# A linear-attention block feeding a GELU MLP on one core: state decay applied block by block, diagonals of the first units by selector matmuls, and a new instruction order

## The chip, the cores and the metric

One core of one Trainium2 chip. The metric is the time of one execution in device microseconds (us). The kernel before takes 191.64 us, the median of 3 runs (191.53 to 192.08). A program on one core has no second core to compare with, so "slow" here is only said of a run that is over 1.5% above the fastest of its kernel; the ratios below use the fast runs.

## The reference

Two stages, shortened:

```python
B, H, S, D = 4, 8, 768, 48            # attention: per (batch, head) a state of D x D
for t in range(S):
    cur = einsum('bhd,bhe->bhde', u * k[t], v[t])
    y[t] = einsum('bhd,bhde->bhe', r[t], state + cur)
    state = w[t][:, :, :, None] * state + einsum('bhd,bhe->bhde', k[t], v[t])
x = y.transpose(0, 2, 1, 3).reshape(B * S, H * D)      # 3072 x 384
h = x @ w_in                                            # 384 x 2048
out = (0.5 * h * (1 + tanh(c * (h + 0.044715 * h**3)))) @ w_out
```

## The kernel before

The recurrence is done in chunks: 12 *units* (three windows of 256 steps for each of 4 batches). A unit q goes through about 40 kinds of small steps; each is a Python function that issues one or a few instructions. A long list of words, `ORDER`, fixes the order in which the steps are issued, and thereby the order on every engine: `mm1.4.2@6` is group 2 of the first projection of unit 4, into PSUM bank 6; a trailing `.A`, `.D` or `.P` picks ScalarE (ACT), VectorE (DVE) or GpSimd (POOL). Each engine gets its own list in this order and waits for what it needs from the others (the longest wait of PE on another engine in the kernel before: 1.4 us, for `rq` on DVE).

The steps that matter here:

```python
def am(q, c2, e):         # the decay of a half unit, spread over a tile that is zero off the two head blocks
    POOL.tensor_tensor(out=t, in0=blk..., in1=st["al", q][:, :, c2]...broadcast, op=AL.mult)   # [128, 384] fp32
def sa(q, c2, e):         # add the old state to the state products p
    DVE.tensor_tensor(out=p2, in0=p2, in1=state[b, 2 * wi + c2 - 1], op=AL.add)
def sm(q, c2, e):         # new state = p * masked decay (also clears the blocks between two heads)
    DVE.tensor_tensor(out=t, in0=st["p", q][c2], in1=st["am", q, c2], op=AL.mult)
def dI(q, n, e):          # POOL puts the diagonal (sum of r*u*k) into the score tile sc
    POOL.tensor_tensor(out=<diagonal blocks of sc>, in0=eye..., in1=d..., op=AL.mult)
def mk(q, n, j, e):       # DVE copies the masked scores mt over it; y = sc^T v follows on PE
    DVE.copy_predicated(sc..., mask..., mt...)
# ... loads, ww/ln/cum/ez/ex (decay sums), kk/rq (scaled k and r), T (transposes), p, y, a5,
# ... xs/X/Xc (output turned), mm1 -> h, gl (gelu), mm2 -> o, ob, store   [cut]
```

Of the kernel before, what the change touches and what calls it, by code (L numbers as in the profile page):

```python
# [21 lines left out]
NG = 2  # L22

ORDER = """
const.0 const.3.D load.w.0 clr.lw.2.D load.w.1 clr.rq.0.P clr.lw.0.P clr.sc.0.P clr.lw.1.P
clr.kk.1.D clr.rq.1.P clr.kk.0.P load.k.0 clr.sc.1.D const.2.D clr.sc.3.D ww.0.P load_u ln.0
ww.1.D kw.0.D load.k.1 rka.0.P ln.1 clr.kk.2.D load.r.0 load.r.1 warm.21@0 cum.0@01 ez.0
kk.0.0 clr.sc.2.D ex.0 cum.1@23 ez.1 kk.0.1 kw.1.D kk.1.0 rka.1.P ex.1 clr.rq.2.D kk.1.1
warm.17@4 T.0.0@4 al.0 const.1.A rq.0.0 warm.12@5 T.1.0@5 rw.0.D rw.1.D rkb.0.D Tc.0.0.A
load.k.2 rq.0.1 load_win.0 rq.1.0 rkb.1.P warm.21@6 T.0.1@6 al.1 dg.0 dI.0.0 load.v.1  # L30
Tc.0.1.A rq.1.1 warm.9@7 T.1.1@7 mt.0.0@04 load.v.0 Tc.1.0.D dI.0.1 am.0.0 load.w.2 vb.0.A
dg.1 mt.0.1@21 p.0@63 dI.1.0 mk.0.0.0 mk.0.0.1 mk.0.1.0 warm.8@5 y.0.0@50 mk.0.1.1 vb.1.A
Tc.1.1.A dI.1.1 mt.1.0@47 load_win.1 sm.0.0 warm.2@2 y.0.1 mk.1.0.0 mt.1.1@21 mk.1.0.1
xs.0.0.A a5.0.1 load.r.2 mk.1.1.0 xs.0.1.A mk.1.1.1 load.v.2 ww.2.P X.0.0@6 am.1.0 X.0.1
Xc.0.D am.0.1 sa.0.1 p.1@45 y.1.0@07 sm.1.0 kw.2.P ln.2 y.1.1 cum.2@21 mm1.0.2@6 a5.1.1 ex.2
load.w.3 sm.0.1 rw.2.P mm1.0.1@4 load_wout.0 xs.1.0.D rka.2.P rkb.2.P ez.2 mm1.0.3@3 rq.2.0
xs.1.1.A kk.2.0 X.1.0@7 al.2 kk.2.1 X.1.1 gl.0.2 mm1.0.0@0 rq.2.1 T.2.0@2 am.1.1 T.2.1@6
gl.0.3 Tc.2.0.A Xc.1.D mm1.1.0@1 gl.1.0 mm1.1.3@7 Tc.2.1.D load.k.3 gl.0.0 mm1.1.1@3 sa.1.1
load.w.4 am.2.0 dg.2 mm1.1.2@2 dI.2.1 mm1.1.7@6 load.r.3 gl.1.1 mt.2.1@10 gl.1.2 mm1.0.4@3
sm.1.1 gl.1.3 load_wout.1 gl.0.1 mk.2.1.0 mt.2.0@27 mk.2.1.1 mm1.0.7@5 load.k.4 gl.0.4 dI.2.0  # L40
mm1.1.6@4 vb.2.A gl.0.7 am.2.1 mk.2.0.0 mm1.1.4@3 mm1.0.5@1 gl.1.6 mm1.1.5@5 p.2@04 ww.3.P
rka.3.P mm1.0.6@2 mk.2.0.1 gl.0.5 sm.2.0 y.2.0@17 gl.1.5 sa.2.1 y.2.1 gl.1.4 gl.1.7 a5.2.1
xs.2.0.A mm2.1.0.0@5 mm2.0.1.0@0 gl.0.6 mm2.0.0.0@3 mm2.0.0.1 mm2.1.1.0@6 mm2.1.0.1 X.2.0@1
kw.3.P ln.3 mm2.0.0.2 sm.2.1 mm2.0.1.1 xs.2.1.D ww.4.P mm2.0.1.2 mm2.1.1.1 cum.3@47 X.2.1
ez.3 Xc.2.A mm2.1.0.2 mm2.1.1.2 al.3 mm2.1.1.3 mm2.0.1.3 rw.3.P mm2.0.0.3 mm2.1.0.3 ex.3
mm1.2.0@2 load.r.4 mm1.2.2@1 rkb.3.P mm2.0.1.4 gl.2.0 mm2.0.0.4 mm2.1.0.4 kk.3.0 mm2.0.1.5
mm2.1.1.4 kk.3.1 rq.3.0 mm2.0.0.5 rq.3.1 load.w.5 dg.3 Td.3.0 kw.4.P mm1.2.3@2 mm2.0.0.6
mm2.1.0.5 mm1.2.5@4 gl.2.2 mm2.0.1.6 mm2.1.1.5 T.3.1@1 am.3.0 am.3.1 rw.4.P ln.4 gl.2.3
cum.4@72 gl.2.5 dI.3.1 mm2.0.0.7 Tc.3.1.D al.4 ex.4 ez.4 mm1.2.7@4 load.v.3 mm2.0.1.7
load.w.6 kk.4.0 mm1.2.1@1 ob.0.0.A load.v.4 kk.4.1 dI.3.0 rka.4.P gl.2.7 mm2.1.1.6 load.r.5  # L50
mm2.1.0.6 ww.5.P ob.0.1.D mm1.2.6@3 rkb.4.P mm2.1.1.7 mm2.1.0.7 load.k.5 mm1.2.4@7 gl.2.6
gl.2.1 mt.3.0@04 rq.4.0 rq.4.1 mt.3.1@23 ob.1.0.A mm2.2.0.0@1 am.4.0 vb.3.A ob.1.1.D
mm2.2.1.0@6 Td.4.0 mk.3.0.0 mm2.2.1.1 rw.5.P mm2.2.0.1 mk.3.0.1 mm2.2.0.2 store.0.1 gl.2.4
p.3@50 ww.6.P mm2.2.1.2 ln.5 y.3.0@74 mk.3.1.0 mm2.2.0.3 mk.3.1.1 mm2.2.1.3 Td.4.1 sm.3.0
y.3.1 a5.3.1 mm2.2.1.4 vb.4.A store.0.0 mm2.2.0.4 xs.3.0.A kw.5.P cum.5@23 sa.3.1 mm2.2.1.5
store.1.0 ex.5 X.3.0@5 xs.3.1.D p.4@74 load.w.7 X.3.1 dg.4 mm2.2.1.6 load.r.6 am.4.1 load.k.6
rka.5.P mm2.2.0.5 mm2.2.0.6 mm2.2.1.7 store.1.1 sm.3.1 mm2.2.0.7 dI.4.1 Xc.3.D al.5 ez.5
mm1.3.1@0 rq.5.0 load.w.8 sa.4.0 sm.4.0 mm1.3.0@5 dI.4.0 ob.2.1.A mm1.3.6@6 kk.5.0 gl.3.0
rq.5.1 mm1.3.2@7 gl.3.6 kk.5.1 mt.4.1@32 ob.2.0.D gl.3.2 ww.7.P rkb.5.P mm1.3.3@5 mm2.3.0.0@6
gl.3.1 mm1.3.7@1 rw.6.P gl.3.3 mk.4.1.0 mm2.3.1.0@7 mk.4.1.1 mt.4.0@05 mk.4.0.0 mm1.3.4@3  # L60
load.v.5 kw.6.P mm2.3.0.1 rka.6.P ln.6 mm1.3.5@2 mm2.3.0.2 mk.4.0.1 rkb.6.P Td.5.1 gl.3.4
mm2.3.0.3 y.4.0@05 Td.5.0 gl.3.5 y.4.1 a5.4.0 a5.4.1 mm2.3.1.1 mm2.3.0.4 cum.6@32 xs.4.1.D
mm2.3.1.2 xs.4.0.A mm2.3.1.3 gl.3.7 mm2.3.1.4 mm2.3.0.5 X.4.0@0 X.4.1 vb.5.P mm2.3.1.5
mm2.3.1.6 mm2.3.0.6 sa.4.1 Xc.4.D am.5.1 mm2.3.0.7 dg.5 load.r.7 ob.3.0.D mm2.3.1.7 al.6
mm1.4.0@5 dI.5.0 load.k.7 mm1.4.5@1 ex.6 sm.4.1 mm1.4.7@0 load.r.8 ln.7 mm1.4.1@6 ez.6 kk.6.0
kk.6.1 rq.6.0 dI.5.1 dg.6 store.2.1 store.2.0 gl.4.5 rq.6.1 mt.5.1@43 mm1.4.6@1 ob.3.1.D
mk.5.1.0 gl.4.7 gl.4.1 Td.6.0 ww.8.P rw.7.P am.5.0 mm1.4.3@0 mm1.4.2@6 mt.5.0@27 gl.4.0
gl.4.3 mk.5.0.0 mk.5.0.1 Td.6.1 mm2.4.1.0@5 mm2.4.1.1 mm1.4.4@4 mm2.4.0.0@0 mk.5.1.1 gl.4.2
p.5@62 mm2.4.0.1 dI.6.1 mm2.4.1.2 mm2.4.1.3 gl.4.4 y.5.0@74 y.5.1 gl.4.6 sa.5.0 a5.5.0
cum.7@31 load.k.9 mm2.4.1.4 mm2.4.1.5 ex.7 sm.5.0 load.v.6 xs.5.0.D a5.5.1 rka.7.P mm2.4.0.2  # L70
rq.7.0 mm2.4.1.6 ez.7 kw.7.P mm2.4.1.7 sa.5.1 X.5.0@6 kk.7.0 al.7 load.k.8 am.6.1 load.w.9
mm2.4.0.3 xs.5.1.A am.6.0 rkb.7.P kk.7.1 load.v.7 X.5.1 mm2.4.0.4 mt.6.1@74 sm.5.1 mm2.4.0.5
Xc.5.A vb.6.P Td.7.0 mm2.4.0.6 mk.6.1.0 mm2.4.0.7 dI.6.0 mm1.5.4@3 mt.6.0@26 rq.7.1 ln.8
Td.7.1 gl.5.4 kw.8.P load.k.10 ob.4.1.A mm1.5.1@7 mk.6.1.1 load.k.11 mm1.5.5@1 mm1.5.0@4
mk.6.0.0 mk.6.0.1 gl.5.5 gl.5.1 gl.5.0 ob.4.0.D p.6@35 sa.6.0 load.r.9 mm1.5.3@1 mm1.5.2@2
sm.6.0 rka.8.P dg.7 y.6.0@76 y.6.1 cum.8@40 a5.6.0 a5.6.1 mm2.5.0.0@3 mm2.5.0.1 gl.5.2
xs.6.0.D mm1.5.6@2 gl.5.3 mm2.5.1.0@1 xs.6.1.D ex.8 X.6.0@7 X.6.1 sa.6.1 ww.9.P mm2.5.1.1
mm2.5.0.2 dI.7.1 mm2.5.0.3 rq.8.0 mm1.5.7@6 mm2.5.0.4 mm2.5.1.2 load.w.10 mm2.5.1.3 al.8
rkb.8.P rw.8.P ez.8 gl.5.6 dI.7.0 sm.6.1 Xc.6.D mm1.6.1@5 vb.7.P am.7.1 mm1.6.2@7 kw.9.P
load.r.11 gl.5.7 ln.9 rq.8.1 kk.8.0 am.7.0 dg.8 am.8.0 gl.6.2 mt.7.0@26 mm2.5.0.5 mm2.5.1.4  # L80
mm1.6.0@0 mm2.5.0.6 mk.7.0.0 store.3.1 gl.6.1 kk.8.1 mm1.6.4@2 mm1.6.7@4 rka.10.P gl.6.0
rw.9.P mm2.5.0.7 mt.7.1@75 mm2.5.1.5 mk.7.1.0 mm1.6.5@0 mk.7.0.1 gl.6.4 gl.6.7 mm2.5.1.6
mm1.6.3@2 mk.7.1.1 mm1.6.6@4 load.v.8 y.7.0@76 store.3.0 rka.9.P mm2.5.1.7 gl.6.5 y.7.1
gl.6.6 ww.10.P ob.5.1.A ob.5.0.D p.7@05 a5.7.0 Td.8.0 mm2.6.0.0@4 dI.8.0 gl.6.3 mm2.6.0.1
mm2.6.0.2 kw.10.P load.v.9 sa.7.0 cum.9@31 load.w.11 mm2.6.1.0@2 ez.9 xs.7.0.A mm2.6.0.3
sm.7.0 store.4.0 load.r.10 a5.7.1 Td.8.1 mm2.6.0.4 xs.7.1.D mm2.6.1.1 mm2.6.1.2 mm2.6.0.5
rkb.9.P X.7.0@0 X.7.1 store.5.0 mm2.6.1.3 sa.7.1 ex.9 ln.10 rq.9.0 al.9 rq.9.1 Xc.7.A
cum.10@76 kk.9.0 ex.10 mm2.6.0.6 mm2.6.0.7 ez.10 kk.9.1 ob.6.0.D rq.10.0 al.10 mm2.6.1.4
mm1.7.0@1 sm.7.1 kk.10.0 kk.10.1 mm2.6.1.5 mm1.7.3@0 kw.11.P dg.9 mm1.7.2@3 vb.8.P mm1.7.5@4
rw.10.P dI.8.1 rq.10.1 ww.11.P mt.8.0@57 gl.7.0 store.4.1 mm2.6.1.6 mk.8.0.0 gl.7.2 mm1.7.1@1  # L90
gl.7.3 mm1.7.4@3 gl.7.1 mm1.7.6@0 mt.8.1@65 am.9.0 gl.7.5 gl.7.4 mm1.7.7@1 mm2.7.0.0@4
mk.8.0.1 mk.8.1.0 mm2.7.1.0@7 mk.8.1.1 mm2.7.1.1 p.8@3 dI.9.0 Td.9.1 Td.9.0 mm2.6.1.7
mm2.7.0.1 gl.7.6 sa.8.0 vb.9.A mt.9.0@06 sm.8.0 gl.7.7 y.8.0@51 mk.9.0.0 rkb.10.P mm2.7.0.2
mk.9.0.1 mm2.7.1.2 load.v.10 y.8.1 a5.8.1 mm2.7.0.3 mm2.7.0.4 ln.11 a5.8.0 rw.11.P ob.6.1.A
mt.9.1@30 mm2.7.0.5 mm2.7.1.3 xs.8.1.D xs.8.0.A dI.9.1 cum.11@26 mk.9.1.0 mk.9.1.1 load.v.11
X.8.0@1 rka.11.P p.9@5 ex.11 sa.9.0 rkb.11.P X.8.1 mm2.7.1.4 mm2.7.0.6 rq.11.0 sm.9.0
mm2.7.1.5 ez.11 kk.11.0 y.9.0@30 y.9.1 mm2.7.1.6 Xc.8.A mm2.7.0.7 a5.9.1 mm1.8.6@1 kk.11.1
a5.9.0 al.11 dg.10 store.5.1 dI.10.1 mm1.8.2@5 xs.9.1.D store.6.0 vb.11.P gl.8.6 mm1.8.4@2
mm2.7.1.7 mm1.8.5@1 gl.8.4 mm1.8.1@0 xs.9.0.A Td.10.0 mm1.8.0@2 gl.8.5 p.11@3 vb.10.P Td.10.1
gl.8.2 ob.7.0.D rq.11.1 dg.11 X.9.0@4 p.10@6 mm1.8.3@1 X.9.1 mm1.8.7@5 gl.8.1 ob.7.1.A  # L100
# [24 lines left out]
def kernel(  # L125
# [87 lines left out]
    def consts_d(e):  # L213
# [3 lines left out]
        DVE.memset(ones2[64:P, 1:2], 1.0)  # L217

    st = {}
    state = {}  # L220

    def tdh(ap):
        return ap.rearrange("p h (t d) -> p t h d", t=2)
# [356 lines left out]
```

## Time and profile before

| | before |
|---|---|
| time | 191.64 us |
| first h matmul starts | 25.97 us |
| h stream of unit 1 starts (PE full from here) | 31.11 us |
| last o matmul ends | 186.2 us |

The order of time of PE (start, duration, engine, line, operation, operands, count; in brackets the idle time before it and what ended it) in the kernel before, at the end of the fill:

```profile
25.97 0.82 PE L481 MATMUL h<-xT,w_in_sb 128*128 128x256 bf16 x6
...
30.67 0.61 PE L321 MATMUL T<-ident,rq 128*128 128x128 bf16 x8 [0.71 <-ACT g L487]
31.11 3.44 PE L481 MATMUL h<-xT,w_in_sb 128*128 128x256 bf16 x30
```

Matmul durations overlap (30.67 + 0.61 is past 31.11), so the starts are what to read. I call what lies ahead of 31.11 the *fill* and what follows the *full part*.

The groups that the change touches, in the kernel before (count, then busy us and mean ns of one, then idle time before them and what ended it):

```profile
L361 POOL TENSOR_TENSOR sc<-eye,dg 128x512 bf16<-128x512 bf16 x24 | 24.8, 1046 | 9.0 <-DVE dg L355 4.6 <-PE y L448 4.4
L378 POOL TENSOR_TENSOR am<-blk,al 128x384 f32<-128x384 bf16 x20 | 16.4, 833 | 0.0
L440 DVE TENSOR_TENSOR S<-p,am 128x384 bf16<-128x384 f32 x20 | 10.9, 552 | 1.5 <-PE p L426 1.0
```

### The profile page before, as it was taken

The numbers are of one execution on the slowest core, as the hardware profiler recorded it, in microseconds if no ns is written. First come the engines' busy times: TensorE is split into PE (matmuls) and PEld (weight loads), VectorE is DVE, ScalarE is ACT, GpSimd is POOL, SyncE is SP. The second block draws the span as 40 slices with busy tenths as digits, with TensorE's granted clock in tenths as the row PEclk, the third lists the DMA queues.
The fourth block names the chain that finished last, engine by engine and source line by source line (L and its number), as shares of the span: only waits on it lengthen the run. The fifth ranks groups of instructions, "written<-read, shape, count | busy, mean of one in ns | idle before, by whom it ended". The sixth has DMA issues, their size and how long they took to land.

```text
span 189.9 us, 5383 instructions
## 1 busy us (share of the span) xinstructions
PE 180.5 (95%) x2258; PEld 131.1 (69%) x2258; DVE 106.3 (56%) x197; ACT 126.8 (67%) x217; POOL 122.7 (65%) x126
## 2 busy tenths in 40 slices
PE   7796988999999999999999999999999999999992
PEld 5574677776776677686587776775687776768760
DVE  3589995662339783696778635977766406020001
ACT  2562649987999689966679969876494442626451
POOL 7394999997996959699499999699277000000000
PEclk9999999999999999999999999999999999999999
DMA  6999999999499799796997999979805600012023
GB/s 148 265 261 235 266 180 258 208 248 216 84 278 226 141 274 208 162 277 106 265 196 137 268 263 175 211 185 268 98 2 132 106 0 3 0 34 94 0 90 117
DMA packets 74919, 31.73 MB, mean 167 GB/s; under 512 B 68880, under 2 KB 74128, under 8 KB 74896
## 3 DMA queue, kind: packets, MB, share of 16 engines
q1 hardware_dynamic: 72016, 28.26, 72.8%
q0 software_dynamic: 2880, 3.15, 9.9%
q8 instruction: 17, 0.28, 0.6%
q14 instruction: 6, 0.05, 0.1%
HBM read 25.36 MB, written 4.72 MB: 158 GB/s over the span
## 4 chain that ended last, share of the span: by engine, by line
PE 83%; DVE 5%; DMA 4%; SPq 3%; ACT 2%; issue 1%; DVEq 0%; ACTq 0%
PE o L494 33%; PE h L481 32%; PE mt L391 4%; DMA r<-in_r_dram 4%; PE y L413 3%; PE p L426 2%; SPq L233 2%; PE y L448 2%; PE Xp L465 2%; DVE sc L398 2%; DVE rk L350 1%; PE T L321 1%; PE x L275 1%; PE z L270 1%; PE dummy L256 1%
## 5 line engine op out<-in xcount | busy, mean ns | idle before, releaser
L494 PE MATMUL o<-w_out_sb,g 128*128 128x384 bf16 x384 | 75.6, 326 | 0.0
L481 PE MATMUL h<-xT,w_in_sb 128*128 128x256 bf16 x576 | 72.3, 273 | 0.0
L487 ACT ACTIVATE g<-h 128x512 bf16<-128x512 f32 x96 | 53.3, 597 | 23.0 <-PE h L481 22.3
L481 PEld LDWEIGHTS <-w_in_sb 128*128 128x128 bf16 x576 | 55.1, 98 | 11.2
L494 PEld LDWEIGHTS <-g 128*128 128x128 bf16 x384 | 34.9, 98 | 16.9
L398 DVE CAST_PREDICATED sc<-mask,mt 128x512 bf16<-128x512 uint16 x48 | 30.7, 684 | 21.6 <-PE mt L391 18.5
L361 POOL TENSOR_TENSOR sc<-eye,dg 128x512 bf16<-128x512 bf16 x24 | 24.8, 1046 | 9.0 <-DVE dg L355 4.6
L344 POOL TENSOR_TENSOR rk<-k,u_bc 128x768 f32<-128x768 f32 x12 | 22.1, 1842 | 3.1 <-DMA u_bc<-in_u_dram 3.1
L350 POOL TENSOR_TENSOR rk<-rk,r 128x768 f32<-128x768 f32 x11 | 20.0, 1820 | 0.3
L378 POOL TENSOR_TENSOR am<-blk,al 128x384 f32<-128x384 bf16 x20 | 16.4, 833 | 0.0
L546 ACT ACT_TABLE_LOAD x12 | 15.4, 1283 | 0.9 <-PEq L563 0.7
L503 DVE COPY ob<-o 128x384 f32<-128x384 f32 x12 | 6.6, 552 | 16.7 <-PE o L494 15.8
L548 ACT ACT_TABLE_LOAD x12 | 15.4, 1283 | 0.2
L256 PE MATMUL dummy<-warm_src 128*128 128x256 bf16 x90 | 13.2, 307 | 1.1 <-DVE ones L215 1.1
L457 DVE CAST xs<-y 128x384 bf16<-128x384 f32 x11 | 6.0, 554 | 12.4 <-PE y L448 12.4
L261 POOL TENSOR_TENSOR ww<-w 128x384 f32<-128x384 f32 x11 | 11.0, 1001 | 2.6 <-DMA w<-in_w_dram 2.6
L434 DVE TENSOR_TENSOR p<-p,S 128x384 f32<-128x384 f32 x16 | 9.0, 561 | 5.4 <-PE p L426 3.9
L294 POOL TENSOR_TENSOR kw<-k,w 128x384 f32<-128x384 f32 x10 | 10.0, 1002 | 2.8 <-DVE kk L306 1.6
L440 DVE TENSOR_TENSOR S<-p,am 128x384 bf16<-128x384 f32 x20 | 10.9, 552 | 1.5 <-PE p L426 1.0
L355 DVE TENSOR_REDUCE dg<-rk 128x16 f32<-128x768 f32 x12 | 11.3, 944 | 0.6 <-POOL rk L350 0.6
L256 PEld LDWEIGHTS <-warm_src 128*128 128x128 bf16 x90 | 9.5, 109 | 3.1 <-DVE ones L215 1.1
L300 POOL TENSOR_TENSOR rw<-r,w 128x384 f32<-128x384 f32 x10 | 10.0, 1000 | 1.7 <-DMA r<-in_r_dram 1.7
(74 smaller groups left out, 188.9 us busy)
## 6 DMA issues: line engine op xcount, KB each, us to landing
w<-in_w_dram SPq DMA_DIRECT2D x12, 384.0 KB, 6.3
k<-in_k_dram SPq DMA_DIRECT2D x12, 384.0 KB, 5.7
r<-in_r_dram SPq DMA_DIRECT2D x12, 384.0 KB, 6.1
v<-in_v_dram SPq DMA_DIRECT2D x12, 384.0 KB, 5.8
out_dram<-ob SPq DMA_DIRECT2D x24, 192.0 KB, 2.5
w_in_sb<-in_moe_w_in_dram POOLq DMA_DIRECT2D x2, 768.0 KB, 9.5
w_out_sb<-in_moe_w_out_dram POOLq DMA_DIRECT2D x2, 768.0 KB, 11.3
T<-kk SPq DMA_TRANSPOSE x18, 4.1
```

The lines of the kernel that those rows point to most:

```text
L256: PE.matmul(t[:, 0:256], warm_src[:, 0:P], warm_src, start=True, stop=True)
L344: ENG[e].tensor_tensor(out=t, in0=st["k", q].rearrange("p h (t d) -> p h t d", t=2), in1=u_bc[:, :, None, :].broadcast_to([P, H, 2, D]), o ...
L350: ENG[e].tensor_tensor(out=t, in0=t, in1=st["r", q].rearrange("p h (t d) -> p h t d", t=2), op=AL.mult)
L355: DVE.tensor_reduce(out=t, in_=st.pop(("rk", q)), axis=AX.X, op=AL.add)
L361: POOL.tensor_tensor(out=bass.AP(tensor=o.tensor, offset=o.offset, ap=[list(o.ap[0]), [256, 4], [192, 2], [1, 64]]), in0=eye[:, None, None ...
L378: POOL.tensor_tensor(out=t, in0=blk.rearrange("p g j d -> p g (j d)"), in1=st["al", q][:, :, c2][:, :, None].broadcast_to([P, G, 2 * D]), ...
L398: DVE.copy_predicated(scs[q % NSC][n][:, :, j].rearrange("p a b c i -> p a (b c i)"), mask.rearrange("p a b t -> p (a b t)").bitcast(U16)[ ...
L481: PE.matmul(h[:, f, :], w_in_sb[i * NWI // 8][:, cb, ts((2 * i + f) % (NFT // NWI), P)], xt[:, :, cb, :], start=(f + cb == 0), stop=(cb == ...
L487: ACT.activation(out=t, in_=st.pop(("h", q, i)), func=AF.Gelu_apprx_tanh)
L494: PE.matmul(st["o", q, c2], st["g", q, i][:, f, ts(c2, P)], w_out_sb[i * NWO // 8][:, (2 * i + f) % (NFT // NWO), :], start=(i + f == 0), ...
L546: ACT.preload_act_table_set(EXP_SET)
L548: ACT.preload_act_table(AF.Gelu_apprx_tanh)
```

## The change

The intent: take work off POOL and DVE in the fill. The decay is applied directly to the two head blocks of each state tile, in tiles cleared once, so `am` goes. For units 0 and 1 the diagonal is no longer written into the score tile: POOL scales v (`vsc`) and PE adds it to y through a diagonal selector (`sel`), so the masks need not wait. Then the order was searched anew, in stages.

```diff
-    def am(q, c2, e): ...                                   # 20 POOL products gone
+    def vsc(q, e):
+        POOL.tensor_tensor(out=t, in0=st["vb", q], in1=<st["dg", q] broadcast over D>, op=AL.mult)
+    def sel(q, e):
+        for t2 in range(2):
+            for c2 in range(2):
+                rows = ds(64 * c2, 64)
+                PE.matmul(st["y", q][c2], diag[rows, t2, :, :]..., st["vsc", q][rows, t2, :, :],
+                          start=False, stop=False, skip_group_check=True)
     def sa(q, c2, e):
-        DVE.tensor_tensor(out=p2, in0=p2, in1=state[b, 2 * wi + c2 - 1], op=AL.add)
+        for j in range(2):
+            rows, cols = ds(64 * j, 64), ds(j * D, D)
+            DVE.tensor_tensor(out=p2[rows, :, cols], in0=p2[rows, :, cols], in1=s[rows, :, cols], op=AL.add)
     def sm(q, c2, e):                                       # likewise: p2 * decay, into the cleared tile s
...                                                          # clears of the state tiles and of all of sc
-ORDER = """ const.0 const.3.D load.w.0 ...                  # 1000 words
+ORDER = """ const.3.D const.2.D clr.kk.0.D clr.S.3.D ...    # 986 words, all in a new order
```

In the new order, among much else: r.0 is loaded ahead of k.1; the 2.56 us product `rkb.0` and `rw.1` move from DVE to POOL; `T.3.0` and `T.4.0` are done by PE instead of the DMA.

## The prediction

> **What bounds the kernel now.** I read the page first (busy shares and the 40 slices), then the table of engine time in chosen stretches, then the chain that ended last in order of time, and last the order of time of the first 31 us.
>
> ```profile
> span 189.9 us, 5383 instructions
> ...
> PE   7796988999999999999999999999999999999992
> ...
> DVE  3589995662339783696778635977766406020001
> ...
> POOL 7394999997996959699499999699277000000000
> ```
>
> One slice is 4.75 us. PE is full from the seventh slice (28.5 us) to the last but one. Before that it is not, and part of what it does there is warm-up matmuls. DVE and POOL are at nine tenths just in the slices where PE is not yet full.
>
> ```profile
> core 0: us, PE busy (x) PEld busy (x) DVE busy (x) ACT busy (x) POOL busy (x), PEclk, DMA share, GB/s
> ...
> 20.00:28.00 8.00, 7.36 (x167) 5.58 (x160) 8.00 (x16) 4.07 (x8) 7.81 (x10) 1.00 1.07 226
> ...
> 31.30:60.00 28.70, 28.70 (x332) 21.31 (x331) 14.58 (x26) 25.96 (x42) 25.79 (x24) 1.00 1.10 214
> 60.00:90.00 30.00, 30.00 (x422) 21.24 (x421) 21.23 (x39) 24.19 (x38) 26.39 (x25) 1.00 1.06 196
> 90.00:120.00 30.00, 29.61 (x389) 21.12 (x387) 20.00 (x37) 23.48 (x40) 25.74 (x23) 1.00 1.14 220
> ```
>
> So there are two regimes. From 31.3 us PE has at most 0.4 us of gaps in 30; POOL (88%) and DVE (70%) only have to keep up. From 20 to 28 us DVE never rests (8.00 of 8.00) and POOL hardly does. The clock is full throughout.
>
> ```profile
> 6.06 7.12 DMA r<-in_r_dram
> 13.20 0.56 DVE rw L300
> 13.76 2.48 DVE rk L350
> 16.24 0.47 DVE rq L312
> ...
> 30.67 0.61 PE T L321 x8
> 31.27 3.28 PE h L481 x30
> ...
> 181.97 4.24 PE o L494 x26
> ...
> 186.28 0.49 ACT ob L501
> ```
>
> The chain says the same: r lands at 13.18, then DVE work (rw, the 2.5 us product rk, rq), transposes, masks and state on DVE, until the first projection (h, then o) takes over. From 31.27 to 186.21 it is PE nearly without a break: 154.9 us of PE work. A tail of 3.7 us (copy, store, end) follows. The measured time is 1.7 us over the span (191.64 against 189.9).
>
> My sum of that PE work: 384 o matmuls at 0.1625 (twelve in 1.95), 552 h at 0.109 (six in 0.655), 20 mt blocks at 0.35, 10 y at 0.51, 10 p at 0.44, 18 state blocks at 0.17, 10 Xp at 0.34, 9 cumulative sums at 0.43, one T at 0.44: 150.0. The other 4.9 is mostly some 41 switches from row-split matmuls back to full ones at about 0.1 (six h are 0.76 after an mt, 0.655 otherwise). **So the time is (start of full PE) + 155 + 3.7 + 1.7, and only an earlier start or less PE work can shorten it.**
>
> [...]
> - [...]am 833 ns / 384 = 2.17, the diagonal 1046 / 512 = 2.04, rk 1842 / 768 = 2.4.
> - [...]16 p matmuls of 96 columns took 0.44 us[...].
> - [...]Here the input loads land every 1.5 us or so (384 KB at the 260 GB/s of 10 to 15 us) until POOL issues the first weight load at 12.59; the two halves of w_in then took 8.8 and 10.2 us.
>
> **The change, part by part.**
> 1. *am goes.* 20 x 833 ns = 16.4 us off POOL, nearly all in the full-PE regime: worth nothing there.
> 2. *sa and sm are split in two halves of 64 partitions.* DVE 36 times: [...]a half is 0.35 and a pair 0.70. +0.15 x 36 = +5.4 us of DVE, in about 130 us in which it is 70% busy: absorbed. In the fill it is 4 pairs, +0.6.
> 3. *Units 0 and 1 get their diagonal by vsc and sel.* Four dI go (4.2 us of POOL), two vsc come: 768 x 2.04 to 2.17 ns = 1.6 us each, 3.2. The masks (mk) of these units no longer wait for dI. sel is 4 matmuls of 384 columns in two row groups: 0.33 to 0.65 us of PE per unit, in the fill.
> 4. *The order of the fill.* DVE loses rkb.0 (2.56), rw.1 (0.56), Tc.1.0 (0.68), Xc.0 (0.54): 4.3 us; POOL takes the first two (1.84 + 1.0). r.0 is loaded ahead of k.1. Full clears of sc and the S tiles lie on DVE and POOL before 8 us, where both wait for loads.
> 5. *The full-PE part.* Two more PE transposes in place of DMA ones (T.3.0, T.4.0): 2 x 0.44 = +0.9. Counting the order, switches go from 41 to 38: -0.3. Everything else on PE is the same count.
>
> *Walk through the new fill*, in each engine's own order with the durations of before. r.0 lands about 10.2 (the fifth load's place), k.1 12.1, r.1 13.2. DVE: rw.0, rq.0 to 11.8; kw.1, kk.1 to 13.7; rq.1.0 14.2; rq.1.1 (after POOL's rw.1, 13.2 to 14.2) 14.8; dg.0 15.7. In before dg.0 and rq.1.1 end at 18.0 and 18.5. Then eight masks at 0.62, dg.1 at 0.95 and two sm at 0.7: the last mask about 22.4, sm.1.0 23.1. POOL: rw.1 to 14.2, w_in issue 15.1, rka.1 and rkb.1 18.8, vsc.0 20.4, ww.2 21.4, second w_in issue 22.2, vsc.1 23.8. sel.1 must wait for that, so the first h matmul is at about 24.5 (25.97 before): **POOL, through vsc.1, becomes what the fill ends on.** After it: three h groups (2.0), Xp (0.34), the fourth h group (0.66), two T (0.9), which puts the h stream of unit 1 at 28.4. That holds if k.2 lands by 25.5; as the twelfth load I put it at 26 (before, the eleventh landed at 23.9), so kw.2, kk.2 and Xc.1 end at 28.7. Start 28.8 in place of 31.27, at the same set of finished PE work: -2.5. Before also lost 0.7 us there to a T waiting for a bank behind the table load; the new banks avoid it.
>
> Sum: -2.5 + 0.9 - 0.3 = -1.9. I give back 0.2 for small new gaps: 191.6 - 1.7 = **189.9 us**, 0.9% faster.
>
> **The rivals.**
> - *The weights take the place of the wait removed.* The first w_in load moves from 12.59 to about 14.2 behind POOL's rw.1, and took up to 10.2 us: 24.4, just when it is needed. The second half (issued about 21.4) is needed at 31, w_out (issued about 27, 11.3 us) at 38.6. All three have under 1 us of slack. For: DMA runs at 200 to 270 GB/s throughout the fill. Against: before, the same loads had 1 to 3 us to spare. If it holds, 190.5 to 191.8.
> - *POOL's relief or the selector saves more.* If vsc runs at 1.2 us, or the inputs land sooner, PE could be full at 26 to 27: 187 to 188.5. Against: POOL has only 0.2 us of idle from 20 to 28 us already and its list until vsc.1 stays as long.
> - *DVE, with 36 more instructions, opens gaps in the full-PE part.* For: 70% average hides peaks, such as the 120 to 150 stretch at 21.3 of 30. Against: the order was searched with these costs, and before has almost no gap. 191 to 193.
>
> **Range and chances.** The start of the full part is uncertain by 1.5 us either way, the gaps by about 1. 8 in 10: 187.8 to 191.7. Over 2% faster needs less than 187.8, a start near 26.6: 0.10. Over 2% slower needs 4 us of new gaps in an order made to avoid them: 0.02. Within 2%: 0.88.
>
> **What would show it.** The chain of the changed kernel should turn to PE without a break at 28 to 29 us; the first h matmul should be at 24 to 25, released by POOL's vsc.1 through sel; vsc 1.6 us, the halves 0.35; PE work from there to the end about 155.5. Wrong if PE waits for a w_in or w_out DMA, if the full-PE stretches show over 1 us of idle in 30, or if sel's matmuls start long before they could by my POOL list.

## The result and the profile after

The changed kernel takes 190.03 us (189.74 to 190.47, 4 runs) against 191.82 us of before on the same chip (191.53 to 192.08). The ratio is 0.9909, interval 0.9883 to 0.9935. Here and below, a ratio is the mean time of one kernel's fast runs over that of before's in the same rounds, so it is not quite the ratio of the medians. On two more chips (experiments e0_after and e11_after_again) it was 0.9868 and 0.9883.

The page of the changed kernel, span and slices; then its table of engine time by stretch:

```profile
span 188.6 us, 5443 instructions
...
PE   7789899999999999999799999999999999999992
...
POOL 8389989658399997949499677993063000000000
...
```

```profile
20.00:28.00 8.00, 7.34 (x120) 5.60 (x120) 7.72 (x17) 5.51 (x11) 7.38 (x9) 1.00 1.13 234
...
60.00:90.00 30.00, 30.00 (x398) 22.55 (x396) 25.27 (x52) 24.10 (x40) 25.50 (x21) 1.00 1.05 205
90.00:120.00 30.00, 28.61 (x411) 21.01 (x409) 22.85 (x48) 24.52 (x43) 23.53 (x22) 1.00 1.17 208
```

PE is at nine tenths from the sixth slice on (23.6 us); before, from the eighth. DVE is still nearly full from 20 to 28 us, and at 60 to 90 us its work rose from 21.23 to 25.27 of 30. In slice 20 of PE there is a 7: a gap of 1.39 us, where before had one of 0.39 in 90 to 120. The order of time of PE in the changed kernel shows the two new starts and that gap:

```profile
24.29 2.14 PE L498 MATMUL h<-xT,w_in_sb 128*128 128x256 bf16 x18
...
28.15 4.09 PE L498 MATMUL h<-xT,w_in_sb 128*128 128x256 bf16 x36
...
93.14 0.52 PE L435 MATMUL p<-vb,kk 64*128 64x96 bf16 x16 [1.39 <-POOL vb L373]
```

The first h matmul comes at 24.29 (25.97 before), full PE at 28.15 (31.11): -2.96 us. The last o ends at 185.1 (186.2): -1.1. So the full part is 1.9 us longer: 1.1 of gaps (1.39 and one of 0.13, against 0.39) and 0.8 of work. Without its gaps the full part is 154.70 us of PE work in before and 155.41 to 155.47 in four profiles of the changed order (after, e0_after, e11_after_again, e7_vsc_twice), so about 0.7 more.

What the fill ends on is seen best in the chain of the changed kernel's second look (e0_after; start, duration, what):

```profile
21.41 0.80 POOL w_in_sb L244
22.22 0.02 issue
22.24 1.51 POOL vsc L378
23.74 0.04 issue
23.79 0.50 PE y L388 x4
24.29 0.28 PE y L465 x4
24.56 1.97 PE h L498 x18
```

That is POOL's `vsc.1`, then the selector, then the state part, then the first h without a break. The new groups of the changed kernel:

```profile
L448 DVE TENSOR_TENSOR p<-p,s 64x192 f32<-64x192 f32 x32 | 11.7, 367 | 5.8 <-issue 2.6 <-PE p L435 2.2
L456 DVE TENSOR_TENSOR s<-p,al 64x192 bf16<-64x192 f32 x40 | 14.2, 354 | 1.5 <-PE p L435 0.7
...
L378 POOL TENSOR_TENSOR vsc<-vb,dg 128x768 bf16<-128x768 bf16 x2 | 3.0, 1488 | 0.0
```

A half costs 0.354 us where a whole cost 0.552 (`sm`), and 0.367 where a whole cost 0.561 (`sa`): by my estimate from these, each instruction carries about 0.16 us that does not shrink with its size (2 x 0.354 - 0.552), and a split pays it twice.

### The profile page after: what moved, and what is told of

Read it like the earlier page. It is cut to its first block, busy times and chain, and to the rows that moved or that the text cites.

```text
span 188.6 us, 5443 instructions
## 1 busy us (share of the span) xinstructions
PE 179.8 (95%) x2273; PEld 131.2 (70%) x2273; DVE 112.9 (60%) x232; ACT 129.2 (69%) x225; POOL 109.6 (58%) x105
## 4 chain that ended last, share of the span: by engine, by line
PE 72%; DMA 11%; SPq 8%; POOL 4%; DVE 1%; ACT 1%; issue 1%; POOLq 0%; ACTq 0%
PE o L511 32%; PE h L498 27%; SPq L233 7%; DMA k<-in_k_dram 6%; DMA v<-in_v_dram 3%; PE mt L400 3%; PE y L422 3%; DMA r<-in_r_dram 2%; PE p L435 2%; POOL rk L350 2%; PE Xp L482 2%; PE y L465 2%; POOL rk L344 1%; SPq L525 1%; PE x L275 1%; PE T L321 1%
## 5 line engine op out<-in xcount | busy, mean ns | idle before, releaser
L511 PE MATMUL o<-w_out_sb,g 128*128 128x384 bf16 x384 | 74.6, 327 | 0.0
L504 ACT ACTIVATE g<-h 128x512 bf16<-128x512 f32 x96 | 53.1, 608 | 29.4 <-PE h L498 28.3
L350 POOL TENSOR_TENSOR rk<-rk,r 128x768 f32<-128x768 f32 x12 | 21.9, 1826 | 3.0 <-DMA r<-in_r_dram 2.7
L361 POOL TENSOR_TENSOR sc<-eye,dg 128x512 bf16<-128x512 bf16 x20 | 20.5, 1041 | 4.5 <-DVE dg L355 4.5
L448 DVE TENSOR_TENSOR p<-p,s 64x192 f32<-64x192 f32 x32 | 11.7, 367 | 5.8 <-issue 2.6
L456 DVE TENSOR_TENSOR s<-p,al 64x192 bf16<-64x192 f32 x40 | 14.2, 354 | 1.5 <-PE p L435 0.7
L373 POOL CAST vb<-v 128x768 bf16<-128x768 f32 x6 | 4.9, 820 | 13.3 <-PE y L422 9.0
L256 PE MATMUL dummy<-warm_src 128*128 128x256 bf16 x81 | 11.3, 295 | 1.1 <-DVE ones L216 1.1
L518 ACT ACTIVATE ob<-o 128x384 f32<-128x384 f32 x15 | 7.3, 490 | 7.0 <-PE o L511 6.8
L520 DVE COPY ob<-o 128x384 f32<-128x384 f32 x9 | 5.0, 554 | 10.9 <-PE o L511 10.9
L312 DVE TENSOR_TENSOR rq<-r,x 128x384 bf16<-128x384 f32 x12 | 6.6, 551 | 6.1 <-ACT x L284 6.0
```

Source lines behind the costliest of these rows:

```text
L350: ENG[e].tensor_tensor(out=t, in0=t, in1=st["r", q].rearrange("p h (t d) -> p h t d", t=2), op=AL.mult)
L361: POOL.tensor_tensor(out=bass.AP(tensor=o.tensor, offset=o.offset, ap=[list(o.ap[0]), [256, 4], [192, 2], [1, 64]]), in0=eye[:, None, None ...
L448: DVE.tensor_tensor(out=p2[rows, :, cols], in0=p2[rows, :, cols], in1=s[rows, :, cols], op=AL.add)
L456: DVE.tensor_tensor(out=s[rows, :, cols], in0=p2[rows, :, cols], in1=st["al", q][rows, :, c2][:, :, None].broadcast_to([64, G, D]), op=AL. ...
L504: ACT.activation(out=t, in_=st.pop(("h", q, i)), func=AF.Gelu_apprx_tanh)
L511: PE.matmul(st["o", q, c2], st["g", q, i][:, f, ts(c2, P)], w_out_sb[i * NWO // 8][:, (2 * i + f) % (NFT // NWO), :], start=(i + f == 0), ...
```

## The experiments

The theory: the gain is an earlier start of the full part, which the fill allows once the masks of units 0 and 1 need no diagonal, with POOL (through `vsc.1`) as what the fill ends on. Rivals: POOL's relief by the missing `am` pays by itself in the full part; the new order alone does it; the weights' landing is what bounds the start; and the new gap near 92 us costs part of the gain.

| run | edit | median us (fast and slow) | ratio to before (fast) |
|---|---|---|---|
| e0_after | changed kernel | 189.18 | 0.9868 ± 0.0014 |
| e1_v6 | v.6 loaded 18 us earlier | 189.34 | 0.9876 ± 0.0016 |
| e2_t34dma | both transposes back to the DMA | 198.45 | 1.0325 ± 0.0046 |
| e3_v6_t34dma | both of these | 196.08 | 1.0249 ± 0.0050 |
| e4_state_alone | before + state part only | 195.33 | 1.0154 ± 0.0070 |
| e5_sel_alone | before + selector only | 191.96 | 1.0023 ± 0.0054 |
| e6_dI | changed, diagonal as before | 195.29 | 1.0170 ± 0.0050 |
| e7_vsc_twice | changed, `vsc` run twice | 193.08 | 1.0061 ± 0.0050 |
| e11_after_again | changed kernel | 189.73 | 0.9883 ± 0.0020 |
| e8_win1_late | changed, w_in half after `vsc.1` | 191.48 | 0.9947 ± 0.0034 |
| e10_am | changed, state part undone | 192.52 | 1.0038 ± 0.0024 |
| e13_t3dma | one transpose back to the DMA | 192.32 | 0.9987 ± 0.0044 |

The runs came in three lots (e0 to e3, e4 to e7, the rest), each on one chip; the numbers e9 and e12 are not on record. All gave the right result. In the first and third the unedited changed kernel ran beside the others; the second is set against it through the ratio to before.

**e0_after, the yardstick.** No edit.

> The changed kernel again, unedited, as the yardstick for the three kernels beside it on the same chip. Expected from the four runs so far: 190.0 us, 0.991 of before, and in its profile one wait of PE of about 1.4 us near 92 us (the state products of unit 6 behind the cast of v.6). Rival: that wait fell only in the one execution that was profiled (188.6 us span, the others 187.3 to 188.3), and is then mostly absent here.

189.18 us, 0.9868. The wait behind v.6 was 0.29 us in its profile. The rival of the expectation holds for most of it: the 1.39 us belong to the execution that was profiled first; in e11 it was 0.50. A gap at this place is in every look, and its length varies (in e11 the chain runs through the landing of v.6, in e0 it does not). The second yardstick, e11_after_again, was expected at 189.1 to 190.1 us, 0.986 to 0.991 of before, with the first h at 24.3 to 24.4; it came at 189.73, 0.9883 and 24.43.

**e1_v6.**

```diff
- ... load.w.7 ... gl.3.2 load.v.7 gl.3.3 ... mm2.4.1.1 load.v.6 xs.5.0.A
+ ... load.w.7 ... gl.3.2 load.v.6 gl.3.3 ... mm2.4.1.1 load.v.7 xs.5.0.A
```

> The loads of v.6 and v.7 exchange places in the order, so that v.6 is issued about 18 us earlier (near 68 us instead of 86). If the one PE gap of 1.4 us comes from the late issue of v.6, it goes and the time falls by 0.8 to 1.4 us against the unedited changed kernel, to about 189 us. Rival: the wait moves to v.7 or to another load, and the time stays within 0.3 us.

189.34 us against 189.18: nothing gained. The wait on v.6 is gone from its profile, and a wait of 0.2 us on a transposing DMA stands in its place. With the yardstick's gap at 0.29 us, there was little to win on this chip.

**e2_t34dma and e3_v6_t34dma.**

```diff
- T.3.0@3 Tc.3.0.D ...            T.4.0@1 ... Tc.4.0.D
+ kk.3.1 Td.3.0 ...               kk.4.1 Td.4.0        # DMA transposes, right after their source
```

> The two transposes that the new order gives to PE (kk of units 3 and 4) go back to the DMA, each issued right after its source is written; two PSUM-to-SBUF copies on DVE go with them. If PE work in the full part counts one for one, the time falls by 0.8 to 0.9 us. Rival: the DMA transposes land too late for the matmuls of units 3 and 4 (about 5 us of other PE work lie between) or hold back the loads behind them on the queue, and the time is the same or up to 2 us longer.

> Both edits together. If both gains are independent terms of the PE sum, about 2.0 us less than the changed kernel, 188.0 us. If the transposes by DMA cost elsewhere, no better than the exchange of v.6 and v.7 alone.

198.45 and 196.08 us: by the medians 9.3 and 6.9 us longer than the changed kernel, not shorter. No execution of the two had a full clock (means 0.971 to 0.991). The order of time of PE in e2_t34dma:

```profile
71.80 0.21 PE L399 MATMUL mt<-T,T 48*64 48x128 bf16 x1 [3.96 <-DMA T<-rq]
...
99.67 0.79 PE L434 MATMUL p<-vb,kk 64*128 64x96 bf16 x16 [2.64 <-POOL vb L372]
```

and its table of engine time just after that first wait (the last three columns are granted clock, DMA share and GB/s):

```profile
70.00:72.00 2.00, 0.20 (x1) 0.14 (x2) 1.51 (x4) 0.00 (x0) 2.00 (x3) 1.00 1.21 187
72.00:74.00 2.00, 1.75 (x22) 1.01 (x20) 1.18 (x2) 0.00 (x0) 2.00 (x3) 0.61 1.08 279
74.00:76.00 2.00, 2.00 (x24) 1.39 (x24) 1.25 (x3) 0.60 (x1) 1.82 (x2) 0.54 1.25 274
```

SP, which issues the loads and the DMA transposes, took them in the order of its list here too. The transpose of kk of unit 4 waited there until kk was written (issued at 61.75 us, after a wait of 4.5), and three loads (64.32, 64.94 and 65.62) and the transpose of rq of the same unit, issued at 61.1 in the changed kernel (after), came after it: rq's at 66.9. PE waited 3.96 us for that. Then the granted clock was 0.61 and 0.54 over the next 4 us. So `T.4.0` on PE, about 0.45 us of PE work, buys this wait off (unit 3 is the subject of e13), and here the PE waits cost more than themselves: the two of the profiled run sum to 6.6 us, and that run (198.59) is 9.4 us over the changed kernel's median.

**e13_t3dma.** The transpose of unit 3 alone goes back.

```diff
- T.3.0@3 Tc.3.0.D
+ kk.3.1 Td.3.0
```

> Only the transpose of kk of unit 3 goes back to the DMA (in the run where both went back, PE waited 4 us for the transpose of rq of unit 4, and not for unit 3). If PE work in the full part counts one for one, 0.4 us less than the changed kernel. If the queue order matters again, the same or longer.

0.9987 against 0.9883: 1% longer, though its fastest run (190.52) is within 0.8 us of the yardstick's median. The expected -0.4 us does not show. The profiled run has a wait of 2.44 us behind v.6 where the yardstick has 0.50, and a lowered clock after it (0.94 over 90 to 120 us; the run, 0.988 in the mean, still counts as fast). The traces show where it arose: from issue to landing the load of v.6 took 4.96 us here and 5.64 in e11, but SP issued it at 87.93 instead of 85.56. So SP's list ran 2.4 us late; which of the waits in it makes up the difference is not settled. The two executions of this kernel at full clock, 190.52 and 191.13, are 0.8 and 1.4 us over the yardstick's median, so the difference is not the clock alone.

**e4_state_alone.** Before's order, `am` words removed, four clears added early on DVE, `sa` and `sm` as in the change, the decay tile with 4 buffers in place of 2 (`sm` now reads the decay late).

> One part of the change alone: the kernel before, its order kept, with the state scaled block by block into cleared tiles and without the masked decay products (20 POOL products of 0.83 us gone, 36 DVE instructions more, four clears on DVE while it waits for the first loads; the decay tile gets 4 buffers in place of 2, as the scaling now reads it late). By the sum that PE work alone counts in the full part, no gain there; in the fill 0.6 us more DVE against 2.4 us less POOL, of which nothing ends later there: 191.8 us within 0.5. Rival: POOL's relief of 16 us pays by itself, 1 us or more faster; second rival: DVE opens gaps, 1 us or more slower.

Missed, and the second rival named why: the four fast runs are 193.9 to 196.6 us, 1.5% longer (the one at 196.57 has a clock of 0.991; the three at full clock are 193.9 to 194.1). In its profile the full part starts at 32.49 us (31.11 before): 1.4 us, where I had counted 0.6 for the four split pairs that lie on DVE's list in the fill. Besides the length of the halves, its chain has 0.1 to 0.4 us of issue time between some of them. Two waits of 0.84 and 0.24 us in the full part come on top, where before had one of 0.39. Taken alone, the state part costs.

**e5_sel_alone.** Before's order, `dI` of units 0 and 1 replaced by `vsc` at their places and `sel` after the last y of the unit.

> The other part alone: the kernel before, its order kept, with the diagonal of units 0 and 1 by vsc and sel instead of the four diagonal products. In before the fill ends on DVE, whose list is not shortened by this; masks wait for the diagonal only 1.9 us in all of the kernel. Expected 191.2 to 191.8 us, at most 0.6 us faster. Rival: the selector by itself opens the fill, 1.5 us or more faster.

1.0023: no gain, as expected. The h stream of unit 1 starts at 31.08 us, before's 31.11. In before's order DVE's list sets the end of the fill and the selector does not shorten it.

**e6_dI.** The changed kernel without the selector.

```diff
- ... dg.0 ...  mk.0.0.1 mk.1.0.0 dg.1 mk.1.0.1      (vsc.0 vsc.1 sel.0 sel.1 in their places)
+ ... dg.0 dI.0.1 dI.0.0 ... mk.0.0.1 dg.1 dI.1.0 dI.1.1 mk.1.0.0 mk.1.0.1
```

> The changed kernel with the diagonal of units 0 and 1 made as before (four POOL products ahead of their masks, the second sum on DVE moved ahead of the masks of unit 1) and no selector. If the selector is what lets the new order of the fill work, the masks of unit 0 wait for POOL to 19 us in place of 16.1 and the first h matmul starts 2 to 3 us later than 24.3: time 192 to 193 us, the gain gone. Rival: the reordering alone (loads, products moved from DVE to POOL) carries it, and the time stays within 0.7 us of 190.

Worse than expected: 1.0170, against 0.987 to 0.988 about 5.5 us longer. PE in its profile:

```profile
24.51 0.50 PE L434 MATMUL p<-vb,kk 64*128 64x96 bf16 x15 [1.76 <-DVE sc L406]
...
27.86 2.91 PE L497 MATMUL h<-xT,w_in_sb 128*128 128x256 bf16 x18
```

The first h starts 3.5 us later than in e0_after (24.40). Its 18 matmuls take 2.91 us instead of 2.13, with a granted clock of 0.88 and 0.78 in the stretches 20 to 28 and 28 to 31.3, after PE's waits. All six executions have a mean clock of 0.972 to 0.991, so part of the 5.5 us is the clock and not the order alone. Of the two orders at hand, before's gains nothing from the selector (e5) and the new one, made for the selector, loses without it. Whether a new search without the selector and the state part would have found a part of the gain was not tried.

**e7_vsc_twice.**

```diff
+        for o in (t_extra, t):
             POOL.tensor_tensor(out=o, in0=st["vb", q], ...)
```

> The changed kernel with each vsc run twice (the first into a scratch tile): 1.49 us more POOL work twice in the fill, 3.0 us in all ahead of the second selector. If the fill ends on POOL through vsc.1, the first h matmul starts about 3 us later (27.2) and the time is 2 to 3 us longer, 192 to 193. If instead DVE or the landing of k.2 sets the start of the full part, less than 1 us of it shows.

```profile
26.55 0.50 PE L390 MATMUL y<-vsc,diag 64*128 64x384 bf16 x4 [0.53 <-POOL vsc L380]
...
27.16 2.13 PE L500 MATMUL h<-xT,w_in_sb 128*128 128x256 bf16 x18
```

2.9 us more on POOL (1.44 and 1.50 in its chain) ahead of the second selector move the first h from 24.40 to 27.16 (+2.76), the h stream of unit 1 from 28.25 to 31.01 (+2.76) and the last o from 183.95 to 186.9 (+2.95). So POOL time ahead of `vsc.1` counts nearly one for one, as it must where the fill ends on it. PE's wait of 1.95 us for the first selector was followed by a lower clock (0.79 over 20 to 28 us; six Xp matmuls took 0.82 us at 23.63, where e0 had 0.63), but that was over before `vsc.1` ended at 26.51 (16 y matmuls took 0.37 us at 25.65, as in e0), and PE still waited 0.53 us for it. The three executions at a clock of 0.989 or more took 191.9 to 192.35 us, the other three (0.979 to 0.982) 193.8 to 194.2.

**e8_win1_late.**

```diff
- ww.2.P load_win.1 sm.1.0 X.0.1 clr.kk.2.D vsc.1
+ ww.2.P sm.1.0 X.0.1 clr.kk.2.D vsc.1 load_win.1
```

> The changed kernel with the issue of the second half of w_in moved on POOL from before vsc.1 to after it. vsc.1 then ends 0.8 us earlier. If POOL alone sets the start, the first h matmul comes 0.8 us earlier (23.6) and the time falls by 0.2 to 0.8 us. If the weights have no slack, as the prediction's first rival had it, the half that is needed at 31 us is issued at 23.5 in place of 21.4, lands at 32 to 33, PE waits for it, and the time is 1 to 2 us longer than the changed kernel.

0.9947, 0.6% longer than e11. The profile is of a slow run, so only its start and its first wait are used; its clock was 1.00 up to 33 us and 0.98 in the next one. Its four fast executions (190.1 to 191.7) had a clock of 0.999 or more.

```profile
23.91 2.13 PE L497 MATMUL h<-xT,w_in_sb 128*128 128x256 bf16 x18
...
33.25 2.11 PE L497 MATMUL h<-xT,w_in_sb 128*128 128x256 bf16 x12 [2.29 <-DMA w_in_sb<-in_moe_w_in_dram]
```

`vsc.1` ends 0.9 us earlier than in e11 (22.88 against 23.76), but the first h comes only 0.5 us earlier (24.43 there): PE no longer waits for `vsc.1` and is busy with its own list up to the first h. And it is worth nothing: the half of w_in, issued 1.4 us later, lands at 33.2 and PE waits. So POOL and the weights bound the start nearly together, and the place of the weight load ahead of `vsc.1` is a compromise between them.

**e10_am.** The changed order with `am` back: four in the fill at POOL's gaps or where they delay least, sixteen ahead of their unit's p; `sa` and `sm` whole; no cleared state tiles.

> The changed kernel with the state part undone: the masked decay products back on POOL (20 of 0.83 us, the four of units 0 and 1 put where POOL has a gap or where they delay least, the others ahead of the state products of their unit), sa and sm whole, no cleared state tiles. If POOL work counts only in the fill, where about 1.1 us of it lies ahead of vsc.1 and the products of k, the time is 0.3 to 1.1 us longer than the changed kernel, and the full part is no longer than there. Rival: the relief of POOL in the full part carries the gain, 1.5 us longer or more. Second rival: the whole sa and sm save 5 us of DVE and the time is shorter.

1.0038 against 0.9883: 2.8 us longer, and my expectation of at most 1.1 was wrong. Its table of engine time and its waits of PE:

```profile
60.00:90.00 30.00, 28.93 (x408) 21.50 (x401) 21.77 (x40) 23.02 (x41) 29.67 (x27) 1.00 1.08 209
```

```profile
32.19 1.48 PE L499 MATMUL h<-xT,w_in_sb 128*128 128x256 bf16 x12 [0.51 <-DMA w_in_sb<-in_moe_w_in_dram]
80.89 1.47 PE L499 MATMUL h<-xT,w_in_sb 128*128 128x256 bf16 x12 [1.06 <-ACT xT L489]
102.94 0.36 PE L431 MATMUL y<-vb,sc 64*128 64x48 bf16 x15 [0.83 <-DVE sc L416]
```

The full part starts 0.62 us later (28.89 against 28.27), the expected share. The rest is new: POOL is busy 29.67 us of 30 between 60 and 90 us (25.50 in e11), and PE, without a gap in that stretch in e11, waits. None of the three waits names POOL itself, so here is the chain before the one at 102.94:

```profile
95.86 1.47 POOL am L396 x2
...
99.14 1.06 POOL sc L363
100.20 0.96 POOL rw L302
101.16 1.01 POOL sc L363
102.20 0.70 DVE sc L416
102.94 0.36 PE y L431 x15
```

Ahead of the wait at 80.89 the chain is POOL's too: two `am` (76.06 to 77.63), `sc` and `ww` to 79.60, then on ACT the logarithm of w (`ln`) and, behind it in ACT's list, `xT`. The wait at 32.19 is the second half of w_in, which POOL issued 0.6 us later than in e11. DVE is lighter than in e11 (21.77 against 25.27), so it is not the cause. In the new order the relief of POOL counts in the full part after all. (The sixteen places were not searched, so a good search might hide some of it.)

No version beat the changed kernel.

## Why the prediction was right

Time: 189.9 us predicted, 190.03 measured in the first set and 189.2 to 189.7 on two more chips. That the first set lies within 0.1 us is in part luck: an earlier start than predicted and a longer gap nearly cancelled. By its steps:

- *The end is the start of full PE plus its work.* Right where the full part stays the same: e7 moved the start by 2.76 us and the end by 2.95. Where it opened gaps or changed the work too, the end moved further than the start: e4 1.4 and 2.4, e6 4.3 and 5.4, e10 0.6 and 2.9.
- *The walk through the fill.* First h predicted at 24.5, measured 24.29 to 24.43; vsc 1.6, measured 1.49; the selector 0.33 to 0.65, measured 0.50 (e0); vsc.1's end 23.8, measured 23.5 to 23.75. "POOL, through vsc.1, becomes what the fill ends on": shown by e7, with two limits that e8 shows. Without POOL's wait the first h comes only 0.5 us earlier, and the weights stand right behind, as the first rival had it.
- *Start of the full part 28.8.* It was 28.15 to 28.3. The term that was off is the landing of k.2: put at 26, it was 25.25, and the h stream followed the transposes directly. The saving there was 2.8 to 3.0 us instead of 2.5.
- *Two more transposes on PE, +0.9, and three switches fewer, -0.3.* Right as a sum: "PE work from there to the end about 155.5" measured 155.41 to 155.47, 0.7 more than before. The switches were not tested singly. For unit 4, e2 shows what the transpose on PE avoids; for unit 3 alone, PE did not wait for the DMA transpose, and still nothing was gained (e13).
- *0.2 us for new gaps.* All gaps of the full part sum to 0.29, 0.50 and 1.52 us in three looks at the same kernel, against 0.39 in before: 0.1 less, 0.1 more and 1.1 more. So it was enough in two looks of three. In the first look the gap behind the load of v.6 took back what the earlier start had given beyond the estimate, and there one of the prediction's own signs of being wrong came true: 28.61 us of PE in 30, over 1 us idle. In e0 and e11 it did not (29.70 and 29.50).
- *"am goes: worth nothing there", in the full part.* This step fell for the new order. In before's order e4 showed no gain from it, but e4 split `sa` and `sm` as well and so does not measure `am` alone. The new order uses POOL so closely that putting `am` back costs 1.9 us more of PE waits (e10: 0.51, 1.06 and 0.83, against 0.50 in e11). I read slack from the profile of before and carried it over to an order that no longer has it.
- *5.4 us more DVE, "absorbed".* Half right. The 0.35 put for a half was not shown by any trace of before; it measured 0.354 and 0.367, so 0.16 to 0.17 per pair as worked out, and PE stays full at 84% DVE (25.27 of 30). But in before's order the same split cost 1.4 us in the fill instead of 0.6 (e4).

- *Its sums.* They hold when redone, but for two slips on which the time does not depend. Over 2% slower means 195.5 us, which is 5.6 us of new gaps over its own 189.9, not 4. And the seventh slice of PE is at 8, not full; the sum rightly starts at 31.27.

So the sum was right with a start put 0.5 us too late, and in the first look a gap 1.1 us longer that hid it. What I did not see is that no part has a value of its own: alone, the state part costs 1.5%, the selector gives nothing, and the new order without either is 1.5% to 3% longer than with both.

## What to carry to other kernels

When one engine is gapless to the end, find the moment it becomes full and walk each engine's own list up to it with measured durations: here that gave the start within 0.7 us, and the PE work behind it within 0.1. Do not give a part of a scheduled change a value of its own from the slack of the old schedule; the new schedule spends that slack. And before removing PE work by handing it to an engine that issues its DMAs in the order of a list, look at what stands behind it in that list (SP in e2: the transpose of rq was issued 5.1 us behind one that had waited for kk, and PE waited 3.96 us for it).

## What the traces show of the clock and of the weight loads

- These waits of PE were followed by a lower granted clock: 1.76 us in e6, with other idle time near it (0.88 over 20 to 28 us, 0.78 over 28 to 31.3); 1.95 in e7 (0.79 over 20 to 28); 2.29 in e8 (0.50 from 34 to 37); 2.44 in e13 (0.94 over 90 to 120); 2.64 in e2 (0.50 over 100 to 102) and 3.96 there (0.61 and 0.54 over 72 to 76); 3.9 in e3 (0.89 over 60 to 90). In the stretches with a single wait of 1.39 us (after, 90 to 120) or 1.06 (e10, 60 to 90) it was 1.00. What decides between the two was not shown. Executions without a trace, slow ones of before among them, stay unexplained.
- Half of w_in took 8.8 and 10.2 us from issue to landing in before, where 68880 of 74919 DMA packets were under 512 B, and the half behind `vsc.1` in e8 took 10.39. This load stands right behind POOL at the start of this kernel.
